# Scaling the softmax exponentials instead of the attention output, and turning operands amid the filler, in a banded-attention and MoE kernel

## The chip, the cores and the metric

The kernel runs on one core of a Trainium2 chip. The time is the device time of one execution in microseconds (us). Its engines appear in the profile as PE (matrix multiplications and transposes; PEld is its loading of weights), DVE (vector), ACT (scalar), POOL (GpSimd) and SP (which issues the transfers). Each engine takes its instructions strictly in its own program's order, and waits at an instruction until the semaphores that it names have been raised.

## The reference

Attention over 4 batches, 8 heads, 768 positions and a head size of 64: scores with a bias that falls with distance, kept for 8 global keys and the last 96 positions only, a softmax, and the product with the values. Its output (3072 rows of 512) goes through a mixture of 8 experts, whose gate is normalized by Sinkhorn steps.

```
scores = scale * np.matmul(q, k.transpose(0, 1, 3, 2)) + bias[None]
scores = np.where(keep, scores, -1000000000.0)
a = np.exp(scores - np.max(scores, axis=-1, keepdims=True))
a = a / (np.sum(a, axis=-1, keepdims=True) + 1e-09)
attn = np.matmul(a, v)
...
for e in range(E):
    out += P[:, e:e + 1] * (np.maximum(x @ w1[e], 0.0) @ w2[e])
```

## The kernel before

**Attention** (`Banded`) goes over 8 units of 384 positions (a batch's half). A unit has 4 pairs of heads, so there are 32 pairs `n`; a pair has 3 groups (one tile of 128 queries for two heads each), so there are 96 groups `t`. `unit` takes them two at a time, in six rounds per unit. I number the rounds of a unit 0 to 5. A round issues, in this order:

1. `ahead`: the scores `s_ps` of two groups four ahead of the round's own, and their softmax: on DVE a fused multiply, add and minimum into `p_sb` (L340), on ACT the exponentials with their sums (L344). After a pair's last group come the sum plus epsilon (L347), its inverse (L348), and a copy of it spread over 128 columns, `inv` (L350).
2. `flush`: the products with the values, `o_ps`, of the round before. If a pair ended, DVE multiplies `o_ps` by `inv` (L436), ACT rounds it to `xh` (L437, the tile `x`), and DVE takes the rest `xl` (L438).
3. `turn`: transposes of the round's own two groups into `t_ps`, copied to `pT` by ACT (L367).
4. `between(2)`, `between(1)`, `between(1)`: the round's **filler**. This is matmul work of the mixture's first expert for the unit before (`h_ps`, `y_ps`, and the gate's `g_ps` and `gt_ps`), drawn from a generator in step with the rounds. The argument sets how much is due, so half of it comes by the first call.
5. In rounds 1 and 4 `invert` for two pairs: three transposes each of `inv` into `r_ps`, copied back by DVE (L446). In rounds 0, 2, 3 and 5 `prepare`: a later pair's `q` and `k` are turned into two tiles `tp`, which ACT rounds to `qh` and `kh` (L295) and DVE reduces to `ql` and `kl` (L296).

PE's instructions are kept in program order; the order on ACT and DVE is set when the kernel is built, by a scheduler with a simulated timeline. The filler starts in round 1 of the second unit and takes the same shape in every unit: `y_ps` x6, `g_ps` x8 and `h_ps` x3 in round 1; `h_ps` x9, `gt_ps` x3 (the gate's transposes) and `h_ps` x6 in round 2; `h_ps` x18 in round 3; `h_ps` x12 and `y_ps` x6 in round 4; `y_ps` x12 in round 5 and in round 0 of the next unit.

**Buffers** of PSUM, all in use: `t_ps`, `tp`, `r_ps` and `gt_ps` share the tag "tp" with two buffers, taken in turn; the filler's `h_ps`, `y_ps` and `g_ps` share the tag "fl" with two (in the first unit `tp` and `r_ps` also take "fl"); `o_ps` has two, the scores one for each head. A tile waits until the tile two before it under the same tag has been read for the last time.

After attention come the remaining experts (`pipeline`, from L941 on), which the change doesn't touch: PE multiplies, and the other engines follow.

Of the kernel before, what the change touches and what calls it, by code (L numbers as in the profile page):

```python
# [8 lines left out]
F32 = mybir.dt.float32  # L9
# [3 lines left out]
ALU = mybir.AluOpType  # L13
# [4 lines left out]
P = 128  # L18
# [4 lines left out]
EPS = 1e-9  # L23
UT = 3
# [8 lines left out]
CHUNK = 2  # L33
LAG = 6
FG = 2
GROUPS = (((0, 0), (1, 0)), ((0, 1), (1, 1)), ((0, 2), (1, 2)))
# [79 lines left out]
class Banded:  # L116
# [184 lines left out]
    def scores(self, ts):  # L301
# [19 lines left out]
                    self.pe.matmul(s_ps, lhsT=t[m][0], rhs=t[m][1], start=(m == 0), stop=(m == 2))  # L321
        return s_lists

    def softmax(self, t, s_list):


        nc, D = self.nc, self.D
        n, group = divmod(t, len(GROUPS))
        _, half, g = self.work[n]
        p_sb = self.wrk.tile([P, 2, 2, P], F32, name="p_sb")  # L330
        mx = self.wrk.tile([P, 2], F32, name="mx", bufs=4)
        if group == 0:
            self.sums[n] = self.wrk.tile([P, UT, 2], F32, name="sm", bufs=4)
        sm = self.sums[n]
        views = []
        for u, (j, i) in enumerate(GROUPS[group]):
            h = 2 * g + j
            pv = p_sb[:, u, 0:len(KEYS[half][i])]
            views.append(pv)
            nc.vector.tensor_tensor_reduce(out=pv, in0=s_list[u], in1=self.bias(h, half, i), scale=-(D ** -0.5), scalar=3.0e38,  # L340
                                           op0=ALU.add, op1=ALU.min, accum_out=mx[:, u:u + 1])
        for u, pv in enumerate(views):
            j, i = GROUPS[group][u]
            nc.scalar.activation(out=pv, in_=pv, func=AF.Exp, bias=mx[:, u:u + 1], scale=-1.0,  # L344
                                 accum_out=sm[:, i, j:j + 1])
        if group == len(GROUPS) - 1:
            nc.scalar.add(sm, sm, EPS)  # L347
            nc.vector.reciprocal(out=sm, in_=sm)  # L348
            self.inv[n] = self.wrk.tile([P, UT, P], F32, name="inv", bufs=3)
            nc.scalar.copy(out=self.inv[n].rearrange("p t (j d) -> p (t j) d", j=2),  # L350
                           in_=sm.rearrange("p t j -> p (t j)").unsqueeze(2).broadcast_to([P, 2 * UT, D]))
        return p_sb
# [31 lines left out]
    def unit(self, u, xh, xl, between):  # L384

        NG, per = len(GROUPS), len(GROUPS) * (self.H // 2)
        if u == 0:
            self.load_k(2)  # L390
            self.prepare(0)
            self.load_v(0)
            self.scale_bias(0)
            self.keep_warm(self.ps, "o", WARM0)
            self.ahead(range(0, CHUNK))
            self.prepare(1)
            for g in range(1, self.H // 2):
                self.scale_bias(g)
            for t in range(CHUNK, AHEAD, CHUNK):
                self.ahead(range(t, t + CHUNK))  # L400
            self.prepare(2)
            self.load_v(2)
        for t in range(u * per, (u + 1) * per, CHUNK):
            self.ahead(range(t + AHEAD, t + AHEAD + CHUNK))
            self.flush()
            for t1 in range(t, t + CHUNK):
                n, group = divmod(t1, NG)
                if group == 0:
                    self.outs[n] = self.ps.tile([P, UT, P], F32, name="o_ps", tag="o", bufs=2)
                g = n % (self.H // 2)  # L410
                self.pending.append((n, group, self.turn(t1), self.outs[n], xh[g], xl[g]))
            for c in (CHUNK, 1, 1):
                between(c)
            n = t // NG
            if t % (2 * NG) == CHUNK:
                self.invert(n)
                self.invert(n + 1)
            else:
                self.prepare(n + NG)
        self.idle = None  # L420

    def flush(self):


        ended = None
        for n, group, pT, o_ps, xh, xl in self.pending:
            self.values(n, group, pT, o_ps)
            if group == len(GROUPS) - 1:
                ended = n, o_ps, xh, xl
        self.pending = []  # L430
        if ended is None:
            return
        n, o_ps, xh, xl = ended
        if n % 2:
            self.load_v(n + 3)
        self.nc.vector.tensor_tensor(out=o_ps, in0=o_ps, in1=self.inv.pop(n), op=ALU.mult)  # L436
        self.nc.scalar.copy(out=xh, in_=o_ps)  # L437
        self.nc.vector.tensor_tensor(out=xl, in0=o_ps, in1=xh, op=ALU.subtract)  # L438

# [687 lines left out]
```

## Time and profile before

| what | value |
|---|---|
| median of 3 runs | 2189.63 us (2189.43 to 2190.45) |
| the profiled execution's own time | 2190.28 us |
| its span, first to last instruction | 2188.4 us |
| PE, DVE, ACT, POOL busy | 99%, 61%, 35%, 51% |
| attention with filler under it | about 50 us to 295 us of the span |
| ACT busy from 60 to 295 us | 167.34 of 235 us |

Attention is the first seventh of the span; the rest is the mixture. PE's clock was granted in full throughout. A matmul's busy time overlaps that of the next, so the pace of PE is read from start to start in the timeline, not from the means. A round is recognized in the timeline by its twelve `s_ps`, then `o_ps`, then `t_ps`.

### The profile page before, as it was taken

How to read it: one execution, taken by the hardware profiler on the slowest of the kernel's cores; microseconds unless marked ns; L12 is line 12 of the kernel's file. 1: busy time of each engine (PE TensorE's matmuls, PEld its weight loads, DVE VectorE, ACT ScalarE, POOL GpSimd, SP SyncE). 2: the span in 40 equal slices, each digit the busy share in tenths (PEclk: the TensorE clock that was granted, in tenths of full speed). 3: DMA queues.
4: the chain of work that ended last, by engine and by line, in shares of the span. 5: the costliest groups of instructions: out<-in, count | busy, mean ns of one | idle time of the engine just before them, and what ended most of it. 6: DMA issues, size and time to landing. Idle time of an engine off the chain costs nothing.

```text
span 2188.4 us, 29227 instructions
## 1 busy us (share of the span) xinstructions
PE 2172.6 (99%) x10851; PEld 1807.7 (83%) x10851; DVE 1326.2 (61%) x2342; ACT 758.1 (35%) x1544; POOL 1124.3 (51%) x1053
## 2 busy tenths in 40 slices
PE   8999999999999999999999999999999999999998
PEld 6888888888888888888888888888888888888887
DVE  7555546665665665665666666666566566566565
ACT  7776753322322222223222223223233223222231
POOL 4858565554544544544544545545455545455440
PEclk9999999999999999999999999999999999999999
DMA  6666452111111111171111111111611111111111
GB/s 163 183 168 184 127 176 92 58 49 58 49 49 58 48 51 56 58 260 49 49 57 49 49 59 49 50 57 49 202 58 48 55 52 49 58 49 49 58 39 50
DMA packets 206280, 173.46 MB, mean 79 GB/s; under 512 B 101168, under 2 KB 169264, under 8 KB 206128
## 3 DMA queue, kind: packets, MB, share of 16 engines
q1 hardware_dynamic: 206128, 171.50, 25.3%
q8 instruction: 87, 1.43, 0.3%
q14 instruction: 65, 0.53, 0.1%
HBM read 142.36 MB, written 29.10 MB: 78 GB/s over the span
## 4 chain that ended last, share of the span: by engine, by line
PE 98%; ACT 1%; DVE 1%; DMA 0%; issue 0%; DVEq 0%; SPq 0%; ACTq 0%
PE y_ps L110 46%; PE bank_a L110 11%; PE bank_d L110 11%; PE bank_c L110 11%; PE bank_b L110 5%; PE h_ps L110 3%; PE o_ps L110 2%; PE s_ps L110 2%; PE t_ps L113 2%; PE tp L113 1%; PE r_ps L113 0%; PE g_ps L110 0%; ACT p_sb L344 0%; PE y_ps L736 0%; PE y_ps L735 0%; PE y_ps L737 0%
## 5 line engine op out<-in xcount | busy, mean ns | idle before, releaser
L1022 DVE SCALAR_TENSOR_TENSOR early<-y_ps,pm,early 128x512 f32<-128x512 f32 x672 | 502.9, 749 | 241.4 <-PE y_ps L110 240.9
L595 POOL TENSOR_TENSOR wl<-wsum,wh 128x1280 fp32r<-128x1280 f32 x90 | 266.5, 2961 | 577.3 <-ACT wh L594 577.3
L617 POOL TENSOR_TENSOR wsum<-w1f 128x256 f32<-128x256 f32 x450 | 317.5, 740 | 313.1 <-DMA w1f<-in_moe_w_dram 313.0
L110 PE MATMUL y_ps<-w2h,h_set 128*128 128x512 f32 x1408 | 433.5, 389 | 0.0
L110 PE MATMUL y_ps<-w2h,x 128*128 128x512 f32 x1408 | 433.5, 389 | 0.0
L594 ACT CAST w2h<-w2f 128x1024 fp32r<-128x1024 f32 x90 | 94.8, 1054 | 688.4 <-issue 619.0
L110 PEld LDWEIGHTS y_ps<-w2h,x 128*128 128x128 f32 x1408 | 264.3, 188 | 54.8
L110 PEld LDWEIGHTS y_ps<-w2h,h_set 128*128 128x128 f32 x1408 | 264.3, 188 | 54.8
L110 PE MATMUL y_ps<-w2l,h_set 128*128 128x512 f32 x704 | 274.1, 389 | 0.1
L110 PE MATMUL y_ps<-w2l,x 128*128 128x512 f32 x704 | 273.9, 389 | 0.0
L110 PE MATMUL bank_a<-m,wh 128*128 128x512 f32 x696 | 242.8, 389 | 1.0 <-DVE h_set L667 1.0
L110 PE MATMUL bank_d<-x,wh 128*128 128x512 f32 x696 | 242.6, 389 | 0.0
L110 PE MATMUL bank_c<-x,wh 128*128 128x512 f32 x696 | 242.5, 389 | 0.0
L595 POOL TENSOR_TENSOR w2l<-w2f,w2h 128x1024 fp32r<-128x1024 f32 x90 | 215.9, 2399 | 48.6 <-ACT w2h L594 48.6
L707 DVE TENSOR_TENSOR early<-early,bank_d 128x512 f32<-128x512 f32 x90 | 62.0, 689 | 175.6 <-PE bank_d L110 171.7
L110 PEld LDWEIGHTS y_ps<-w2l,h_set 128*128 128x128 f32 x704 | 132.2, 188 | 27.8 <-DVE early L1022 0.5
L110 PEld LDWEIGHTS y_ps<-w2l,x 128*128 128x128 f32 x704 | 132.2, 188 | 27.4
L110 PEld LDWEIGHTS bank_a<-m,wh 128*128 128x128 f32 x696 | 130.7, 188 | 29.0 <-DVE h_set L667 1.9
L110 PEld LDWEIGHTS bank_c<-x,wh 128*128 128x128 f32 x696 | 130.7, 188 | 27.1
L110 PEld LDWEIGHTS bank_d<-x,wh 128*128 128x128 f32 x696 | 130.6, 188 | 27.0
L110 PE MATMUL bank_a<-m,wl 128*128 128x512 f32 x348 | 135.4, 389 | 0.0
L110 PE MATMUL bank_d<-x,wl 128*128 128x512 f32 x348 | 135.4, 389 | 0.0
(228 smaller groups left out, 3473.6 us busy)
## 6 DMA issues: line engine op xcount, KB each, us to landing
w1f<-in_moe_w_dram SPq DMA_DIRECT2D x92, 512.0 KB, 3.5
w2f<-in_moe_w_dram SPq DMA_DIRECT2D x92, 512.0 KB, 3.3
x<-op_m SPq DMA_DIRECT2D x16, 512.0 KB, 7.4
op_m<-op SPq DMA_DIRECT2D x30, 256.0 KB, 2.5
m<-op_m SPq DMA_DIRECT2D x12, 512.0 KB, 7.0
out_dram<-early SPq DMA_DIRECT2D x24, 256.0 KB, 4.3
ys<-y_sb SPq DMA_DIRECT2D x21, 256.0 KB, 2.9
early<-ys SPq DMA_DIRECT2D x21, 256.0 KB, 4.1
```

The lines of the kernel that those rows point to most:

```text
L110: return self.tc.keep_in_program_order(self.engine.matmul(*args, **kw))
L113: return self.tc.keep_in_program_order(self.engine.transpose(*args, **kw))
L594: self.nc.scalar.copy(out=hi, in_=full)
L595: self.nc.gpsimd.tensor_tensor(out=lo, in0=full, in1=hi, op=ALU.subtract)
L617: nc.gpsimd.tensor_tensor(out=s[:, n], in0=x, in1=y, op=op)
L707: tt(out=t3, in0=t3, in1=d, op=ALU.subtract)
L1022: nc.vector.scalar_tensor_tensor(out=a, in0=y_ps, scalar=moe.pm[:, tt, e:e + 1], in1=a, op0=ALU.mult, op1=ALU.add)
```

## The change

The pairs of the first unit (`n < 4`) stay as they were. For every later pair, each group's two sums get epsilon and are inverted on DVE at once (two instructions on 128x2), and the exponentials themselves are multiplied by the inverse before they are turned: six multiplications per pair, of 128x256 (128x128 in a first group of a batch's first half), two on DVE (the first head of groups 0 and 2) and four on ACT. What they replace for those 28 pairs: the sum plus epsilon and `inv` on ACT, the six transposes per two pairs into `r_ps` on PE and their two copies on DVE, and the multiplication of `o_ps` on DVE.

Second, `prepare` moves from the end of the round to the middle of its filler, after `between(2)`.

```diff
+        early = self.early_pair(n)
+        if not early:
+            sm = self.wrk.tile([P, 2], F32, name="sm2", bufs=8)
+        elif group == 0:
             self.sums[n] = self.wrk.tile([P, UT, 2], F32, name="sm", bufs=4)
-        sm = self.sums[n]
...
-        if group == len(GROUPS) - 1:
+        if not early:
+            nc.vector.tensor_scalar(out=sm, in0=sm, scalar1=EPS, scalar2=None, op0=ALU.add)
+            nc.vector.reciprocal(out=sm, in_=sm)
+            for u, pv in enumerate(views):
+                if u == 0 and group != 1:
+                    nc.vector.tensor_scalar(out=pv, in0=pv, scalar1=sm[:, u:u + 1], scalar2=None, op0=ALU.mult)
+                else:
+                    nc.scalar.mul(pv, pv, sm[:, u:u + 1])
+        elif group == len(GROUPS) - 1:
+            sm = self.sums[n]
...
-            for c in (CHUNK, 1, 1):
-                between(c)
             n = t // NG
-            if t % (2 * NG) == CHUNK:
+            between(CHUNK)
+            if t % (2 * NG) != CHUNK:
+                self.prepare(n + NG)
+            elif self.early_pair(n):
                 self.invert(n)
                 self.invert(n + 1)
-            else:
-                self.prepare(n + NG)
+            between(1)
+            between(1)
...
-        self.nc.vector.tensor_tensor(out=o_ps, in0=o_ps, in1=self.inv.pop(n), op=ALU.mult)
+        if self.early_pair(n):
+            self.nc.vector.tensor_tensor(out=o_ps, in0=o_ps, in1=self.inv.pop(n), op=ALU.mult)
```

PE's order in round 2 of the second unit, before. `gt_ps` are the gate's transposes, `tp` the turned operands, `s_ps` opens the next round:

```order
L110 MATMUL h_ps<-x_174,w1h 128x384
L113 MATMUL gt_ps<-ident,g_sb 128x16 x3
L110 MATMUL h_ps<-x_175,w1h 128x384
L110 MATMUL h_ps<-x_173,w1l 128x384
L110 MATMUL h_ps<-x_173,w1h 128x384
L110 MATMUL h_ps<-x_175,w1h 128x384
L110 MATMUL h_ps<-x_173,w1l 128x384
L110 MATMUL h_ps<-x_173,w1h 128x384
L113 MATMUL tp<-ident,early 128x128 x6
L110 MATMUL s_ps_1146<-kl,qh 128x256
```

The same place in the changed kernel:

```order
L110 MATMUL h_ps<-x_174,w1h 128x384
L113 MATMUL tp<-ident,early 128x128 x6
L113 MATMUL gt_ps<-ident,g_sb 128x16 x3
L110 MATMUL h_ps<-x_175,w1h 128x384
L110 MATMUL h_ps<-x_173,w1l 128x384
L110 MATMUL h_ps<-x_173,w1h 128x384
L110 MATMUL h_ps<-x_175,w1h 128x384
L110 MATMUL h_ps<-x_173,w1l 128x384
L110 MATMUL h_ps<-x_173,w1h 128x384
L110 MATMUL s_ps_1169<-kl,qh 128x256
```

`tp` now stands ahead of `gt_ps`, which in the buffers' turn takes the first of the two `tp` tiles: its wait, which named ACT before, names DVE's `ql` now.

ACT's order in that round, before (`x` is the rounded attention output, `hh` belongs to the filler):

```order
L344 ACTIVATE p_sb,sm<-p_sb,mx 128x256 x4
L367 COPY pT<-t_ps 128x512
L437 CAST x_173<-o_ps 128x3x128
L347 ACTIVATE sm<-sm 128x6
L367 COPY pT<-t_ps 128x512
L666 ACTIVATE hh<-h_ps 128x384
L350 COPY inv<-sm 128x384
L295 CAST qh<-tp 128x384
L295 CAST kh<-tp 128x384
```

And in the changed kernel, where L350 are the exponentials, L453 is the rounding of the output, L382 the copies of `pT`, L359 the multiplications and L682 `hh`:

```order
L350 ACTIVATE p_sb,sm_1053<-p_sb,mx 128x256
L453 CAST x_173<-o_ps 128x3x128
L350 ACTIVATE p_sb,sm_1064<-p_sb,mx 128x256
L350 ACTIVATE p_sb,sm_1053<-p_sb,mx 128x256
L350 ACTIVATE p_sb,sm_1064<-p_sb,mx 128x256
L382 COPY pT<-t_ps 128x512 x2
L359 ACTIVATE p_sb<-p_sb,sm_1053 128x256
L682 ACTIVATE hh<-h_ps 128x384
L359 ACTIVATE p_sb<-p_sb,sm_1064 128x256
L295 CAST qh<-tp 128x384
L295 CAST kh<-tp 128x384
```

The rounding of the output moved ahead of both copies of `pT`, and the two multiplications stand between `pT` and `qh`.

More of the change, by code (lines that the diff above doesn't have):

```diff
@@ L322, in scores, with early_pair @@
         return s_lists
+    def early_pair(self, n):
+        return n < self.H // 2
     def softmax(self, t, s_list):
@@ L331, in softmax @@
         mx = self.wrk.tile([P, 2], F32, name="mx", bufs=4)
-        if group == 0:
+        early = self.early_pair(n)
+        if not early:
+            sm = self.wrk.tile([P, 2], F32, name="sm2", bufs=8)
+        elif group == 0:
             self.sums[n] = self.wrk.tile([P, UT, 2], F32, name="sm", bufs=4)
-        sm = self.sums[n]
         views = []
@@ L344, in softmax @@
             nc.scalar.activation(out=pv, in_=pv, func=AF.Exp, bias=mx[:, u:u + 1], scale=-1.0,
-                                 accum_out=sm[:, i, j:j + 1])
-        if group == len(GROUPS) - 1:
+                                 accum_out=self.sums[n][:, i, j:j + 1] if early else sm[:, u:u + 1])
+        if not early:
[8 more added lines that the diff above has]
+            sm = self.sums[n]
             nc.scalar.add(sm, sm, EPS)
             nc.vector.reciprocal(out=sm, in_=sm)
-            self.inv[n] = self.wrk.tile([P, UT, P], F32, name="inv", bufs=3)
+            self.inv[n] = self.wrk.tile([P, UT, P], F32, name="inv", bufs=2)
             nc.scalar.copy(out=self.inv[n].rearrange("p t (j d) -> p (t j) d", j=2),
```

## The prediction, made before the changed kernel ran

> **What bounds the kernel now.** I read the page first, its busy times and the chain that ended last, then the busy times of the stretch of attention that has filler under it, then the timeline of single rounds.
>
> ```profile
> span 2188.4 us, 29227 instructions
> PE 2172.6 (99%) x10851; PEld 1807.7 (83%) x10851; DVE 1326.2 (61%) x2342; ACT 758.1 (35%) x1544; POOL 1124.3 (51%) x1053
> PE 98%; ACT 1%; DVE 1%; DMA 0%; issue 0%; DVEq 0%; SPq 0%; ACTq 0%
> 60.00:295.00 235.00, 235.00 (x1994) 205.61 (x1990) 126.89 (x464) 167.34 (x526) 167.12 (x195) 1.00 0.59 164
> ```
>
> PE sets the end, and from 60 to 295 us it is never idle; ACT is busy there for 167.34 of 235 us (71%), DVE for 126.89 (54%). So what the change takes off PE is worth its full length, as long as PE still finds everything ready. Whether it does is a matter of single rounds. This is round 2 of a unit on PE, from the `r_ps` that close the round before to the next `s_ps`:
>
> ```profile
> 208.78 0.34 PE L110 MATMUL h_ps<-x,w1h 128*128 128x384 f32 x1
> 208.96 0.82 PE L113 MATMUL r_ps<-ident,inv 128*128 128x128 f32 x6
> 209.71 0.38 PE L110 MATMUL s_ps<-kl,qh 64*128 64x256 f32 x2
> ...
> 210.61 1.09 PE L110 MATMUL o_ps<-pT,early 128*64 128x128 f32 x16
> 211.63 1.09 PE L113 MATMUL t_ps<-ident,p_sb 128*128 128x128 f32 x8
> 212.48 0.42 PE L110 MATMUL h_ps<-x,w1h 128*128 128x384 f32 x1
> ...
> 213.99 0.34 PE L110 MATMUL h_ps<-x,w1h 128*128 128x384 f32 x1
> 214.25 0.35 PE L113 MATMUL gt_ps<-ident,g_sb 16*128 16x16 f32 x3
> ...
> 215.69 0.82 PE L113 MATMUL tp<-ident,early 128*128 128x128 f32 x6
> 216.44 0.39 PE L110 MATMUL s_ps<-kl,qh 64*128 64x256 f32 x2
> ```
>
> and the same round on ACT, and DVE's two rows that matter:
>
> ```profile
> 211.18 0.51 ACT L344 ACTIVATE p_sb<-p_sb,mx 128x256 f32<-128x256 f32 x1 [2.22 <-DVE mx L340]
> 211.69 0.49 ACT L344 ACTIVATE p_sb<-p_sb,mx 128x256 f32<-128x256 f32 x1
> ...
> 213.16 0.57 ACT L367 COPY pT<-t_ps 128x512 f32<-128x512 f32 x1
> 213.63 0.47 ACT L437 CAST x<-o_ps 128x384 fp32r<-128x384 f32 x1
> 214.00 0.21 ACT L347 ACTIVATE sm<-sm 128x6 f32<-128x6 f32 x1
> 214.11 0.57 ACT L367 COPY pT<-t_ps 128x512 f32<-128x512 f32 x1
> 214.57 0.49 ACT L666 ACTIVATE hh<-h_ps 128x384 fp32r<-128x384 f32 x1
> 214.96 0.51 ACT L350 COPY inv<-sm 128x384 f32<-128x384 f32 x1
> 216.22 0.48 ACT L295 CAST qh<-tp 128x384 fp32r<-128x384 f32 x1 [0.75 <-PE tp L113]
> ...
> 210.71 0.42 DVE L340 CUSTOM_DVE_ANT_1 p_sb<-s_ps,early 128x256 f32<-128x256 f32 x1 [0.20 <-PE s_ps L110]
> 216.73 0.56 DVE L296 TENSOR_TENSOR ql<-tp,qh 128x384 fp32r<-128x384 f32 x1 [1.07 <-ACT qh L295]
> ```
>
> What to see: counted from the round's start (209.71), the second `pT` is done at 4.97 us (214.68), `tp` comes at 5.98; a full microsecond of slack. And from `tp`'s start (215.69) it takes until 217.29, 1.60 us, for `qh` and `ql` to have read the first `tp` tile. In the old order the next round's scores and values run in that time.
>
> **The change part by part.** *The transposes of `inv`.* A filler step followed by `r_ps` and `s_ps` takes 208.78 to 209.71, 0.93 us. Without `r_ps` the same passage stands once in the trace, in the last unit, and takes 0.27 us:
>
> ```profile
> 294.65 0.34 PE L110 MATMUL h_ps<-x,w1h 128*128 128x384 f32 x1
> 294.92 0.39 PE L110 MATMUL s_ps<-kl,qh 64*128 64x256 f32 x2
> ```
>
> So 0.66 us for each of the 14 rounds that lose their `r_ps` (two in each of seven units): **-9.2 us**, all of it on the path. This is also all that can be gained, since PE waits for nothing there; what goes from DVE (two copies, one multiplication, one inverse) was hidden behind PE.
>
> *`tp` in mid-filler, ahead of `gt_ps` (round 2).* `tp` takes the two buffers of `t_ps`, and `gt_ps` right behind it takes the first `tp` tile's again, so PE must stand still until `ql` has read it. The floor is in the rows above: 1.60 us after `tp`'s start plus about 0.05 for the signal, where PE needs 0.65 for its six transposes: 1.0 us, if ACT takes `qh` at once. It won't, by its new order: one exponential, `x`, three exponentials, two `pT`, multiplication, `hh`, multiplication, `qh`. I put durations to it. The multiplication by a per-partition number isn't in the trace at this size; the nearest rows are the exponential, with such an operand too, and a rounding from SBUF without one:
>
> ```profile
> L344 ACT ACTIVATE p_sb<-p_sb,mx 128x256 f32<-128x256 f32 x160 | 80.0, 501 | 54.6 <-DVE mx L340 54.4
> L594 ACT CAST wh<-w1f 128x256 fp32r<-128x256 f32 x180 | 63.8, 404 | 0.0
> ```
>
> Between 404 and 501 ns I take 0.50 us, from the one with the operand, and a step of 0.40, because neighbours on ACT overlap by 0.1 (213.16 + 0.57 against 213.63). From the round's start: first exponential at 1.47; `x` at 2.10, when `o_ps` is done; three exponentials at 2.47, 2.96 and 3.45; `pT` at 3.94 and 4.40, done at 4.50 and 4.97; multiplication 4.87, `hh` 5.27, multiplication 5.66, `qh` 6.06 to 6.54, `ql` until 7.13, `gt_ps` at 7.18. PE reaches `tp` after nine `h_ps` at 4.46, is held by both `pT` for 0.24 in all, and reaches `gt_ps` at 5.35. The loss is 0.24 + 1.83 = 2.07 us; with exponentials of 128 columns, in every second unit, the same walk gives 1.74. Six rounds (units 2 to 7 of eight; the last has no operands left to turn) by 1.9: **+11.4 us**. Ends: 6 x 1.0 = 5.8 if ACT were free, and 18 if `qh` came another microsecond later.
>
> *`tp` in the other rounds (3, 5 and 0).* Here the first half of the filler is nine `h_ps` or six `y_ps`. In a round that started at 110.75, the seventh `y_ps`, in whose place `tp` comes now, stood at 4.04 us:
>
> ```profile
> 110.75 0.39 PE L110 MATMUL s_ps<-kl,qh 64*128 64x256 f32 x2
> 114.79 0.39 PE L110 MATMUL y_ps<-w2l,hh 128*128 128x512 f32 x1
> ```
>
> The second tile comes three transposes (0.33) later and needs the second `pT`, which by the steps above ends between 4.65 and 4.91, now that `x` stands ahead of it. That holds PE for 0.2 to 0.55, mean 0.35, in twelve rounds 5 and 0, and for 0.12 in six rounds 3: **+4.9 us**. Ends: 0, and 10 at 0.55 throughout. That PE does wait there when `pT` is late shows once in the first unit, where no filler stands between:
>
> ```profile
> 44.25 1.05 ACT L367 COPY pT<-t_ps 128x512 f32<-128x512 f32 x2
> 44.87 0.55 PE L113 MATMUL tp<-ident,raw_q 128*128 128x128 f32 x3 [1.25 <-ACT pT L367]
> ```
>
> *The multiplications ahead of `y_sb` (round 1).* `h_ps` after the gate's `g_ps` takes the buffer that `y_sb` has to empty. In the round that started at 202.61 this was already to the point:
>
> ```profile
> 207.69 0.58 ACT L894 COPY y_sb<-y_ps 128x512 f32<-128x512 f32 x1
> 208.33 0.44 PE L110 MATMUL h_ps<-x,w1h 128*128 128x384 f32 x1
> ```
>
> Now three multiplications, 1.2 us, stand ahead of `y_sb`, while the exponentials start some 0.4 earlier, because the casts of `tp` are mostly over. `y_sb` ends 0.5 to 0.75 later than `h_ps` needs: 0.6 in seven rounds, **+4.2 us**. Ends: 0 and 5.3.
>
> *The first unit's last rounds* have no filler, and ACT leads there. The second unit's first softmaxes fall into them: eight multiplications (3.2 us) come in, two sums and `inv` go (1.2). I take **+1.5 us**, between 0 and 3.2.
>
> *At nothing*: the small DVE instructions (per pair three sums plus epsilon and three inverses of about 0.18, two multiplications of 0.25 to 0.45, against 1.3 removed: L436, L446 and L348) add 0.5 us to a pair, stay under DVE's 54%, and in the walk they are done before 4.9, ahead of `qh`. The operands' loads are issued half a round earlier on SP, ahead of the spills that the second half of the filler queues; no wait of PE before names a transfer, and each load has two rounds or more. If that cover failed, PE would stand at `tp` for as long as the load is late, in each of 24 rounds.
>
> The sum: -9.2 + 11.4 + 4.9 + 4.2 + 1.5 = **+12.8 us**. The profiled execution took 2190.28 (span 2188.4 and 1.9 around it), 0.65 above the median; added to the median of 2189.63 this makes **2202.4 us**, 0.6% slower. [...]
>
> **The rivals.** *ACT keeps ahead* (same): `pT` and `qh` come as early as in the old order, say because `x` never holds ACT up. Then only the floor is left: -9.2 + 5.8 + about 1 = -2.4, 2187 us. For it: 29% of ACT is idle. Against: the idle time lies at the start of each round, ahead of the first exponential (the 2.22 us in the row), not ahead of `pT`.
>
> *The transposes go, and nothing takes their place* (faster): `gt_ps` doesn't have to wait for `ql`, because the casts finish under PE's own transposes. The place is round 2, the price 0.66 us in 14 rounds, 2181 us; it decides once all new waits together stay under 4.8 us. Against: 1.60 us of `qh` and `ql` cannot pass under 0.65 us of PE.
>
> *ACT becomes the bound*: four multiplications of 0.4 for each pair, less 0.6 for the sum and `inv`, add 1.0 us to a pair's 7.0 (167.34 over the 24 pairs of these six units, of 9.8 us each), 82%. If single rounds overflow into the next, the ends above apply: -9.2 + 18 + 8 + 5.3, about +22, 2212 us. Against: every round ends with idle time on ACT before it.
>
> **How the numbers follow.** Forecast 0.66 (2195 to 2209), ACT keeps ahead 0.16, nothing in the transposes' place 0.12, ACT the bound 0.06. A measurement of this kernel tells 0.2%, 4.4 us, from no change. Faster 0.12 and same 0.16 are the two middle rivals, slower 0.72 the forecast and the last. For 8 in 10 I go down to 2187, the floor's case, and up to 2212, the last's.
>
> **What would show it.** Right: in round 2, PE idle before `gt_ps` for 1 to 2 us, released by `ql`, six times; `tp` held by `pT` for tenths of a microsecond; `h_ps` after `g_ps` held by `y_sb`; PE's busy share from 60 to 295 us below full for the first time; no `r_ps` after 40 us. Wrong: `gt_ps` following `tp` within 0.3 us, or `qh` starting within 0.6 us of `tp`'s start in round 2, and a span that is shorter by about 9 us.

## The result, and the profile after

The changed kernel takes **2223.5 us** (median of 6 runs, 2221.28 to 2224.89), the one before 2189.70 (2189.43 to 2191.05, 6 runs). The ratio is 1.0151, with a 95% interval of 1.0141 to 1.0161: slower by 33.8 us. The forecast was slower too, but by 12.8 us, to 2202.4, with a range up to 2212.

From here on I count against the profiled execution, which took 2221.8 us; its span is 31.6 us longer than the one before (2220.0 against 2188.4). The changed kernel's page, its span, its busy times and its chain:

```profile
span 2220.0 us, 29286 instructions
...
PE 2180.6 (98%) x10767; PEld 1804.0 (81%) x10767; DVE 1378.0 (62%) x2482; ACT 786.0 (35%) x1600; POOL 1123.5 (51%) x1053
...
PE 93%; DVE 3%; ACT 3%; issue 1%; DMA 0%; SPq 0%; DVEq 0%; ACTq 0%
```

and the stretch with filler, in the same columns as before (us, busy times with instructions, then the granted clock):

```profile
60.00:295.00 235.00, 216.88 (x1725) 180.61 (x1726) 153.18 (x520) 167.91 (x506) 143.72 (x162) 0.96 0.52 147
```

PE was busy for all 235 us of this stretch before and is now for 216.88. What has no match in the prediction is the last number but two: the granted clock was 1.00 and is 0.96. The waits of the changed kernel's PE, by what was waited for (us in total, times, longest):

```profile
PE h_ps L110 <- ACT y_sb L910: 8.9, 6, 2.1
PE gt_ps L113 <- DVE ql L296: 8.9, 6, 1.7
PE tp L113 <- ACT pT L382: 5.7, 8, 3.5
```

Places and releasers are the predicted ones: `gt_ps` released by `ql` six times, `tp` by `pT`, `h_ps` by `y_sb`. The size of the first row is not, with waits up to 2.1 us where I had 0.6. Of the third row 3.5 us is a single wait in the first unit's last rounds (at 46.48; the same wait took 1.25 before); the other seven make 2.2.

The table compares every round of the units 1 to 7 with the same round before, by the starts of its `s_ps` in the two traces (us, summed over the units). "Predicted" are the terms of the prediction, put where they belong (the gain from the transposes goes half to round 1 and half to round 4). The other columns are the changed kernel and those experiments that a later section needs.

| round | predicted | changed | scaling alone | move alone | changed, no epsilon | the same, PE kept busy |
|---|---|---|---|---|---|---|
| 0 of unit 1 (no filler yet) | +1.5 | +2.8 | +2.7 | 0.0 | +2.9 | +4.0 |
| 0 (others) and 5 | +4.2 | +5.1 | +0.2 | +3.2 | +5.2 | +5.2 |
| 1 | -0.4 | +7.4 | +2.3 | -0.5 | +1.5 | +1.3 |
| 2 | +11.4 | +16.3 | +5.7 | +7.4 | +13.2 | +11.9 |
| 3 | +0.7 | +4.5 | +3.1 | +0.8 | +6.9 | +1.5 |
| 4 | -4.6 | -4.6 | -4.5 | -0.1 | -4.6 | -4.6 |
| difference of the spans | +12.8 | +31.6 | +9.8 | +10.3 | +25.1 | +19.2 |

**Round 2, where the stall was foreseen.** The rows of PE in the second unit, in a round that started at 55.07:

```profile
60.06 1.02 PE L113 MATMUL tp<-ident,early 128*128 128x128 f32 x6 [0.37 <-ACT pT L382]
62.67 0.37 PE L113 MATMUL gt_ps<-ident,g_sb 16*128 16x16 f32 x3 [1.58 <-DVE ql L296]
```

and ACT and DVE in the same round:

```profile
60.39 0.50 ACT L359 ACTIVATE p_sb<-p_sb,sm 128x256 f32<-128x256 f32 x1
60.80 0.46 ACT L682 ACTIVATE hh<-h_ps 128x384 fp32r<-128x384 f32 x1
61.17 0.49 ACT L359 ACTIVATE p_sb<-p_sb,sm 128x256 f32<-128x256 f32 x1
...
61.57 0.45 ACT L295 CAST qh<-tp 128x384 fp32r<-128x384 f32 x1
...
62.06 0.56 DVE L296 TENSOR_TENSOR ql<-tp,qh 128x384 fp32r<-128x384 f32 x1 [0.20 <-ACT qh L295]
```

Multiplication, `hh`, multiplication, `qh`, `ql`, `gt_ps`: the walk of the prediction, step by step. It had `qh` at 6.06 and `gt_ps` at 7.18 from the round's start; they stand at 6.50 and 7.60, because the exponentials began 0.4 later. The step on ACT is 0.40 (60.39, 60.80, 61.17, 61.57), as taken. But look at the clock in the 3.5 us behind `gt_ps` (the number to read is the third from the end):

```profile
62.90:66.40 3.50, 3.50 (x20) 3.02 (x19) 0.54 (x3) 0.00 (x0) 3.42 (x6) 0.52 0.29 75
```

and at the starts of the six `h_ps` there and of what follows them, in the changed kernel and then at the same place before:

```profile
62.97 0.69 PE L110 MATMUL h_ps<-x,w1h 128*128 128x384 f32 x1
...
65.19 0.58 PE L110 MATMUL s_ps<-kl,qh 64*128 64x256 f32 x2
```

```profile
214.54 0.45 PE L110 MATMUL h_ps<-x,w1h 128*128 128x384 f32 x1
...
215.69 0.82 PE L113 MATMUL tp<-ident,early 128*128 128x128 f32 x6
```

From 62.9 on PE is busy, but at half its clock, for about 3.4 us. The six `h_ps` take 2.22 us there, against 1.15 before and 1.25 in the changed kernel's next unit, where the clock stayed full (108.41 to 109.66). This stall was paid twice: 1.58 us while PE stood, and about 1 us more in the six `h_ps` behind it.

**Round 1, where the stall was three times the foreseen.** The rows of a round that started at 92.16, on DVE, POOL, ACT and PE:

```profile
95.22 1.30 POOL L655 TENSOR_TENSOR xres<-x 128x512 f32<-128x512 f32 x1
...
95.27 1.27 DVE L353 TENSOR_SCALAR sm<-sm 128x2 f32<-128x2 f32 x1 [0.54 <-ACT p_sb L350]
...
96.48 1.29 POOL L656 TENSOR_TENSOR xsum<-x 128x512 f32<-128x512 f32 x1
96.58 0.17 DVE L354 RECIPROCAL sm<-sm 128x2 f32<-128x2 f32 x1
96.78 1.06 DVE L357 TENSOR_SCALAR p_sb<-p_sb,sm 128x128 f32<-128x128 f32 x1
...
97.77 0.15 DVE L353 TENSOR_SCALAR sm<-sm 128x2 f32<-128x2 f32 x1
...
98.16 0.91 ACT L359 ACTIVATE p_sb<-p_sb,sm 128x256 f32<-128x256 f32 x2 [0.91 <-DVE sm L354]
98.97 0.56 ACT L910 COPY y_sb<-y_ps 128x512 f32<-128x512 f32 x1
...
99.59 0.44 PE L110 MATMUL h_ps<-x,w1h 128*128 128x384 f32 x1 [2.08 <-ACT y_sb L910]
```

The sum plus epsilon on DVE, an addition to two numbers per partition, took 1.27 us. It ended at 96.54, where POOL's addition that had started just ahead of it ended too (96.52). The multiplication behind it took 1.06, until POOL's next one was done. The next sum started at 97.77, when POOL had just ended, and took 0.15. The reciprocal beside it took 0.17 each time, whatever POOL did. So it is in the whole trace: of the 84 sums, the 35 that began while POOL was idle took 155 to 171 ns, and the 49 that began while POOL was in an instruction ended 24 to 63 ns after that instruction did. ACT's multiplications waited 0.91 us for the inverse, `y_sb` stood behind them, and PE stood 2.08 us. The groups of these three over the whole run (the count, busy time, mean ns of one):

```profile
L353 DVE TENSOR_SCALAR sm<-sm 128x2 f32<-128x2 f32 x84 | 38.7, 461 | 15.3 <-ACT p_sb L350 14.6
L357 DVE TENSOR_SCALAR p_sb<-p_sb,sm 128x256 f32<-128x256 f32 x44 | 26.7, 608 | 1.3
L354 DVE RECIPROCAL sm<-sm 128x2 f32<-128x2 f32 x84 | 13.9, 165 | 2.6
```

I had put about 0.18 us for the sum and 0.25 to 0.45 for the multiplication. So there were two candidates for the missing 19 us: DVE's new instructions, which seem to wait for POOL, and PE's half pace after a stall.

### The profile page after: what moved, and what is told of

Same layout as the page of the kernel before. It is cut to its first block, busy times and chain, and to the rows that moved or that the text cites. A ratio compares the mean times of both kernels' runs of the same rounds, so it can differ in the third digit from the quotient of the medians.

```text
span 2220.0 us, 29286 instructions
## 1 busy us (share of the span) xinstructions
PE 2180.6 (98%) x10767; PEld 1804.0 (81%) x10767; DVE 1378.0 (62%) x2482; ACT 786.0 (35%) x1600; POOL 1123.5 (51%) x1053
## 4 chain that ended last, share of the span: by engine, by line
PE 93%; DVE 3%; ACT 3%; issue 1%; DMA 0%; SPq 0%; DVEq 0%; ACTq 0%
PE y_ps L110 45%; PE bank_a L110 11%; PE bank_d L110 11%; PE bank_c L110 11%; PE bank_b L110 5%; PE h_ps L110 2%; PE s_ps L110 2%; ACT p_sb L350 1%; PE o_ps L110 1%; PE t_ps L113 1%; PE tp L113 1%; DVE sm L353 1%; DVE p_sb L357 1%; ACT pT L382 0%; DVE p_sb L346 0%
```

## The experiments

The experiments ran in four groups, each beside the kernel before on the same chip (medians of 2190.05 to 2190.62 us there).

### The scaling alone

The operands are turned at the round's end, as before; the scaling is that of the changed kernel.

```diff
             between(CHUNK)
+            between(1)
+            between(1)
             if t % (2 * NG) != CHUNK:
                 self.prepare(n + NG)
...
-            between(1)
-            between(1)
```

> The early scaling alone: the operands are turned at the end of the round again, as before. Theory A (DVE's new instructions that read and write SBUF alone wait for POOL's, and so the copy of y_sb comes late): the removed transposes give -9.2 us, the waits of h_ps for y_sb in round 1 stay at 10 to 12, the first unit costs 3: 2190 to 2200 us, and the small instructions on DVE still take up to 1.3 us. Theory B (ACT's own added work makes y_sb late, as the prediction had it): -9.2 + 4.2 + 1.5, 2186 us.

Measured: 2199.57 us, ratio 1.0039 (1.0025 to 1.0053), in theory A's range, but not by its way. The scaling alone loses 10 us, though it takes 9.2 us of transposes off PE. PE's largest wait in the whole trace, and its place in a round 2:

```profile
PE tp L113 <- issue: 4.3, 2, 2.2
```

```profile
99.13 1.12 DVE L353 TENSOR_SCALAR sm<-sm 128x2 f32<-128x2 f32 x1
...
100.17 1.44 DVE L357 TENSOR_SCALAR p_sb<-p_sb,sm 128x256 f32<-128x256 f32 x1
...
101.71 1.17 DVE L357 TENSOR_SCALAR p_sb<-p_sb,sm 128x128 f32<-128x128 f32 x1
102.80 0.17 DVE L785 COPY lg<-gt_ps 128x24 f32<-128x24 f32 x1
...
103.29 0.63 PE L113 MATMUL tp<-ident,early 128*128 128x128 f32 x4 [2.16 <-issue]
```

Here `y_sb` was in time (the scheduler had put it ahead), where theory A had 10 to 12 us of waits for it. The loss came out elsewhere. The largest piece: the gate's `lg` (L785, L786), which has to empty the buffer of `gt_ps` for the second `tp`, stood on DVE behind three of the new instructions, 1.1 to 1.4 us each. The row names no releaser, so that it is `lg` is read from DVE's order and the times: `tp` starts when `lg`'s two instructions, from 102.80 on, are over. A stretch at half clock follows each of these two stalls (granted clock 0.50 from 104.5 and from 186.4 us on), and `t_ps` waits another 3.7 us for `kl`, behind DVE as well.

### The move alone

`prepare` amid the filler, with the output scaled through `inv` as before and `invert` at the round's end. The edit is against the kernel before:

```diff
-            for c in (CHUNK, 1, 1):
-                between(c)
             n = t // NG
+            between(CHUNK)
+            if t % (2 * NG) != CHUNK:
+                self.prepare(n + NG)
+            between(1)
+            between(1)
             if t % (2 * NG) == CHUNK:
                 self.invert(n)
                 self.invert(n + 1)
-            else:
-                self.prepare(n + NG)
```

> The turning of the operands amid the filler alone, without the early scaling; the inverse sums are turned at the end of their rounds as before. Theory A (PE runs at half pace for some 3.5 us after an idle time of more than about a microsecond): gt_ps waits 1.0 to 1.4 us in six rounds and PE then loses about 1.5 more, tp waits 0.1 to 0.4 in 18 rounds: 2207 to 2213 us, granted clock below full behind each gt_ps. Theory B (the waits are all there is): 2199 to 2203 us.

Measured: 2200.68 us, ratio 1.0049 (1.0032 to 1.0065): theory B held. PE's first wait and the rows of one round 2:

```profile
PE gt_ps L113 <- DVE ql L296: 5.4, 6, 0.9
```

```profile
96.62 1.14 PE L113 MATMUL tp<-ident,early 128*128 128x128 f32 x7
...
97.42 0.49 ACT L295 CAST qh<-tp 128x384 fp32r<-128x384 f32 x1
98.05 0.55 DVE L296 TENSOR_TENSOR ql<-tp,qh 128x384 fp32r<-128x384 f32 x1
...
98.65 0.35 PE L113 MATMUL gt_ps<-ident,g_sb 16*128 16x16 f32 x3 [0.89 <-DVE ql L296]
```

With no multiplication on ACT, `gt_ps` waits 0.9 us each time: the floor of 1.0 that the prediction worked out. The granted clock stays at 1.00 from 60 to 295 us, so a stall of 0.9 us brought no half pace. Each part alone costs 10 to 11 us, together they cost 34; some 14 us come from their meeting.

### The changed kernel without POOL's sums and differences

This one leaves out POOL's additions and subtractions of activations for the later experts, so those experts compute something else; the amount of work on the other engines stays.

```diff
-            moe.combine((new[:, 0], new[:, 1]), block(x, c, n), block(y, c, n), op, xtmp)
-            spills.append((op_spill[b][m][:, :, q], new))
+            spills.extend((op_spill[b][m][:, s, q], block(x, c, n)[s]) for s in range(2))
```

> The changed kernel without POOL's sums and differences of the attention output (the tiles are spilled as they are, so the first layer's operands are not the sums that the mixture needs). Theory A (POOL holds DVE's new instructions up): L353 falls to about 0.17 us and L357 to 0.35, the waits of h_ps for y_sb fall from 9.9 to 4 us or less, the first unit gets 2 us back: 2213 to 2217 us. Theory B (ACT's work alone): 2222 to 2225 us, waits unchanged.

Measured: 2213.71 us, ratio 1.0106 (1.0089 to 1.0123), in theory A's range. The group of the sums, and the wait for `y_sb`:

```profile
L353 DVE TENSOR_SCALAR sm<-sm 128x2 f32<-128x2 f32 x84 | 17.9, 213 | 18.7 <-ACT p_sb L350 17.6
```

```profile
PE h_ps L110 <- ACT y_sb L908: 2.3, 6, 0.6
```

The mean of a sum falls from 461 to 213 ns (the first unit's weights are still made on POOL, under which one of them took 2.3 us), `y_sb`'s waits from 8.9 to 2.3 us, longest 0.6: that is the size that the prediction had for this term. So POOL's work is what made DVE's instructions long, and that made `y_sb` late. 24 us of loss remain, and the half pace with them: round 3 still loses 6.9 us.

### The changed kernel with PE kept busy at the stall

Twelve useless transposes follow `tp` in round 2, into a part of `tp` that nobody reads, so that PE does not stand still before `gt_ps`.

```diff
-    def prepare(self, n):
+    def prepare(self, n, extra=0):
...
+            for _ in range(extra if hi is kh else 0):
+                self.pe.transpose(out=tp[:, 3], in_=src[:, nb - 1], identity=self.ident)
...
-                self.prepare(n + NG)
+                self.prepare(n + NG, 12 if t > 4 * NG and t % (4 * NG) == 2 * CHUNK else 0)
```

> The changed kernel with 12 useless transposes (1.3 us) behind tp in each round 2, in the time in which PE waits for gt_ps anyway; the wait itself still ends with ql. Theory A (PE's half pace follows from its idle time): h_ps behind gt_ps runs at full pace, 1.3 to 1.8 us less in six rounds: 2213 to 2216 us. Theory B (the half pace has another cause): 2222 to 2226 us.

Measured: 2218.59 us, ratio 1.0127 (1.011 to 1.0143), between the two ranges: 5 us less than the changed kernel, with more work on PE, where theory A had at least 7.5. Round 3 lost 1.5 us in place of 4.5, 0.22 to 0.26 in each unit. The stretch with filler:

```profile
60.00:295.00 235.00, 223.41 (x1814) 187.04 (x1813) 153.37 (x528) 170.80 (x516) 144.77 (x163) 0.98 0.53 150
```

The clock is at 0.98 in place of 0.96: the half pace behind `gt_ps` is gone, and two stretches of it remain, each behind a stall of 2.1 us for `y_sb` in round 1.

### All multiplications on ACT

The scaling alone again (operands turned at the round's end), without the sum plus epsilon (a softmax's sum is at least 1, the exponential of its own maximum, so 1e-9 changes no bit of it in fp32), and with DVE's two multiplications of a pair on ACT.

```diff
-            nc.vector.tensor_scalar(out=sm, in0=sm, scalar1=EPS, scalar2=None, op0=ALU.add)
             nc.vector.reciprocal(out=sm, in_=sm)
             for u, pv in enumerate(views):
-                if u == 0 and group != 1:
-                    nc.vector.tensor_scalar(out=pv, in0=pv, scalar1=sm[:, u:u + 1], scalar2=None, op0=ALU.mult)
-                else:
-                    nc.scalar.mul(pv, pv, sm[:, u:u + 1])
+                nc.scalar.mul(pv, pv, sm[:, u:u + 1])
```

> As the scaling alone (operands turned at the round's end again, 2199.57 us), but without the sum plus epsilon (a softmax's sum is at least 1, so 1e-9 changes nothing in fp32), and with all six multiplications of a pair on ACT. DVE keeps only the reciprocal, which took 0.16 us throughout and waited for nobody on POOL. Theory (what the scaling alone loses comes from DVE's two new forms, which wait behind POOL's instruction and hold up lg, ql and the exponentials' scaling): the losses of rounds 1, 2 and 3 go, round 4's gain of 3.9 us stays, the first unit still costs 1 to 3 us: 2186 to 2191 us, and the wait of tp for the gate's buffer in round 2 (4.3 us) is under 1. Rival (ACT's load is the cause: 56 more multiplications of 0.4 us come on to ACT): rounds 1 to 3 lose as much as before or more, with PE waiting for y_sb or pT: 2198 to 2206 us.

Measured: 2205.25 us, ratio 1.0069 (1.0052 to 1.0086). The theory's number fell and the rival's held: rounds 2 and 3 were free of loss (0.0 us each), as the theory had it, but rounds 1, 4 and 0 lost 4.1, 5.4 and 5.5. PE waits at the start of a round now:

```profile
66.39 1.70 ACT L355 ACTIVATE p_sb<-p_sb,sm 128x256 f32<-128x256 f32 x4
...
67.98 0.48 ACT L678 ACTIVATE hh<-h_ps 128x384 fp32r<-128x384 f32 x1
...
68.35 0.48 ACT L295 CAST qh<-tp 128x384 fp32r<-128x384 f32 x1
...
70.69 1.09 PE L113 MATMUL t_ps<-ident,p_sb 128*128 128x128 f32 x8 [1.29 <-DVE ql L296]
```

Four multiplications (1.70 us) stand ahead of `hh` and `qh` on ACT, `ql` then falls behind DVE's work for the next scores, and the next round's `t_ps` finds its buffer still read. So in this order ACT has no room for six multiplications a pair.

### The same on the changed kernel

The same edit of the scaling, with `prepare` amid the filler.

> As the changed kernel (2223.5 us, operands turned amid the filler), with the same edit of the scaling: no sum plus epsilon, all six multiplications on ACT. Theory (two causes that multiply each other: the transposes' place costs 1 to 1.7 us at gt_ps in six rounds, whatever scales the exponentials; DVE's waits behind POOL make y_sb late): the waits for y_sb fall from 8.9 us to under 4, the loss of round 1 from 7.4 to under 3, that of round 2 stays at 10 to 16, since more multiplications stand ahead of qh: 2206 to 2216 us. Rival (ACT's load): no better than the changed kernel, 2222 to 2232 us.

Measured: 2218.98 us, ratio 1.0133 (1.0117 to 1.015), in neither range. `y_sb`'s waits fell to 1.7 us and round 1 lost 0.1 in place of 7.4, as the theory had it, but round 2 lost 18.0, more than its 16: ACT had all six of a pair's multiplications instead of four, and `gt_ps` waited 14.0 us in all, up to 2.5 at a time.

### Only the sum plus epsilon left out

The scaling alone, with one line less.

```diff
-            nc.vector.tensor_scalar(out=sm, in0=sm, scalar1=EPS, scalar2=None, op0=ALU.add)
             nc.vector.reciprocal(out=sm, in_=sm)
```

> As the scaling alone (2199.57 us), with only the sum plus epsilon left out; the two multiplications of a pair on DVE stay. Theory: every sum plus epsilon waits behind POOL's instruction (mean 0.46 us against 0.15 undisturbed, 84 of them), the multiplications too (mean 0.61, 56 of them); taking the first away takes about half of the loss in rounds 1 to 3 away (10 us): 2192 to 2197 us. If only the multiplications matter: 2198 to 2200; if only the sums: 2187 to 2191.

Measured: **2189.72 us**, ratio 0.9997 (0.9988 to 1.0007): 9.9 us less than the scaling alone, as much as that had lost on balance, from one instruction on two numbers per partition. My theory had half; the number is that of its third case, that only the sums matter. The multiplications still wait:

```profile
L356 DVE TENSOR_SCALAR p_sb<-p_sb,sm 128x256 f32<-128x256 f32 x44 | 32.8, 746 | 1.5
```

At 746 ns they are even longer than in the changed kernel (608). The difference, as I read the order of the instructions, is what stands behind: the sum is the first link for all of a group's multiplications, ACT's too, while DVE's own multiplication only holds what DVE has next. That is argued, not tried, and it isn't free everywhere: in the first unit's last rounds two multiplications of 1.56 and 2.25 us stand on DVE ahead of the next scores' work (from 40.16 on), `pT` comes late, and PE waits 3.5 us for it. Round 1 has none of the transposes' gain either. The version that beats both, below, gets both back.

### Another instruction in the sum's place

It could still be any further instruction at that point that costs 10 us. So here a useless reciprocal of the same two numbers, into a scratch tile, stands in the place of the sum.

```diff
-            nc.vector.tensor_scalar(out=sm, in0=sm, scalar1=EPS, scalar2=None, op0=ALU.add)
+            nc.vector.reciprocal(out=self.wrk.tile([P, 2], F32, name="sm3", bufs=8), in_=sm)
             nc.vector.reciprocal(out=sm, in_=sm)
```

> As the scaling alone without the sum plus epsilon (2189.72 us), but with a useless instruction in its place: a reciprocal of the same 128x2 numbers into a scratch tile. So DVE has as many instructions in as long a chain as in the scaling alone (2199.57 us), and only the form differs: a reciprocal took 0.16 us throughout, the sum plus epsilon 0.46 on average, up to 1.25, when POOL was busy. Theory (it is the form, which waits behind POOL): 2189 to 2192 us. Rival (any further instruction between the exponentials and their scaling costs it, by its place in DVE's order): 2197 to 2201 us. Between: both.

Measured: 2189.35 us, ratio 0.9995 (0.9986 to 1.0005). The theory held. The two groups of reciprocals:

```profile
L354 DVE RECIPROCAL sm<-sm 128x2 f32<-128x2 f32 x84 | 13.8, 165 | 2.5
L353 DVE RECIPROCAL sm<-sm 128x2 f32<-128x2 f32 x84 | 13.7, 163 | 22.0 <-ACT p_sb L350 21.1
```

Same size, same count, same place in DVE's order; 163 ns in place of 453, and 10 us of the kernel. One thing differs besides the form: nothing reads this reciprocal's result, while the sum's was the next instruction's input. With that proviso, it is the form of the instruction, together with POOL's work beside it.

### All multiplications on ACT, and y_sb on DVE

```diff
-                    nc.scalar.copy(out=y_sb, in_=y_ps)
+                    nc.vector.tensor_copy(out=y_sb, in_=y_ps)
```

> As e5_scale_act, with y_sb copied from PSUM by DVE, which takes 0.6 us off ACT for each of the first expert's tiles; a copy out of PSUM should not wait for POOL. Theory (DVE's forms were the cause, and ACT is only tight behind pT): no PE wait for y_sb or y_ps, 2182 to 2189 us, below the kernel before by up to 0.3%. Rival (y_sb on DVE waits behind DVE's longer work, as lg did): PE waits at h_ps behind g_ps for 0.5 us or more in each round 1: 2191 to 2196 us.

Measured: 2192.67 us, ratio 1.0012 (1.0002 to 1.0021). With `y_sb` off ACT the kernel is 12.6 us faster than with all multiplications alone, and no wait for `y_sb` is left; rounds 0 lose 1.3 in place of 5.5, and round 1 gains 3.6 where it lost 4.1. But `t_ps` still waits for `ql` behind ACT's multiplications, 7.5 us in six rounds 4, so the theory's range was missed by nearly 4 us. The number lies in the rival's range, but not by the rival's way: `y_sb` is in time.

### A version that beats both

From these: the scaling alone, without the sum plus epsilon, with `y_sb` copied on DVE, and the old way also for the second unit's first two pairs, whose scaling falls into the first unit's rounds where ACT leads.

```diff
     def early_pair(self, n):
-        return n < self.H // 2
+        return n < 3 * self.H // 4
...
-                    nc.scalar.copy(out=y_sb, in_=y_ps)
+                    nc.vector.tensor_copy(out=y_sb, in_=y_ps)
```

> As the scaling alone without the sum plus epsilon (2189.72 us), with two edits more: the old way also for the second unit's first two pairs, whose scaling falls into the first unit's rounds where ACT leads (the loss there was 3.2 + 0.9 + 0.6 us), and y_sb copied from PSUM by DVE, which took 3.6 us off round 1 when all multiplications were on ACT. Theory: the first unit's loss falls to under 1 us, less 0.7 for its r_ps; round 1 gains 2 to 4; round 4's gain of 4 stays: 2181 to 2186 us, faster than the kernel before by 0.2 to 0.4%. Rival (y_sb behind DVE's multiplications, which still wait for POOL, comes late): PE waits at h_ps behind g_ps, 2187 to 2192.

Measured: **2182.60 us** (5 runs, 2182.43 to 2183.13), ratio 0.9966 (0.9952 to 0.9979). The theory held: 0.34% faster than the kernel before, 41 us faster than the changed one. The first unit's loss is gone. The busy times of its page (the span is 2180.5 us):

```profile
PE 2164.4 (99%) x10773; PEld 1799.2 (83%) x10773; DVE 1354.9 (62%) x2415; ACT 773.3 (35%) x1575; POOL 1125.2 (52%) x1053
```

Rounds 1 and 4 have the transposes' gain, -4.4 and -4.6 us; round 2 gives 1.2 back. This is nearly what the rival "the transposes go, and nothing takes their place" had promised (2181), but only with the operands turned at the round's end.

### The changed kernel without the sum plus epsilon

> The changed kernel (2223.5 us) with only the sum plus epsilon left out. Theory (the prediction's terms held, and the sum's wait behind POOL was what they lacked, at y_sb and, by PE's half pace after the longer stalls, behind gt_ps): 2200 to 2208 us, with y_sb's waits under 4 us, gt_ps's at 8 to 11, and a granted clock of 0.99 or more in each round. Rival (the multiplications on DVE, which wait too, or ACT's order are enough for the late y_sb): 2214 to 2222 us.

Measured: 2213.19 us, ratio 1.0103 (1.0088 to 1.0119), between the two ranges. One line less gives 10.3 us back here too. The waits and the clock:

```profile
PE gt_ps L113 <- DVE ql L296: 9.5, 6, 1.7
...
PE h_ps L110 <- ACT y_sb L909: 3.2, 6, 0.6
```

```profile
60.00:295.00 235.00, 221.28 (x1766) 183.59 (x1766) 129.89 (x467) 170.91 (x519) 147.38 (x168) 0.96 0.54 150
```

The waits are those of the theory, 3.2 for `y_sb` and 9.5 for `gt_ps`; its clock is not. I had thought that the half pace would go with the long stalls for `y_sb`. It stays at 0.96, with five stretches after the first unit behind the stalls at `gt_ps` alone, of 1.5 to 1.7 us.

### Both causes taken away

The changed kernel without the sum plus epsilon, and with the twelve useless transposes behind `tp` in round 2.

> The changed kernel without the sum plus epsilon (2213.19 us), and PE kept busy behind tp in round 2 by twelve useless transposes into a part of tp that nobody reads, as in the run with the busy wait alone (2218.59 us against 2223.5 for the changed kernel). Both causes that the prediction lacked are then taken away: the sums' wait behind POOL, and PE's half pace after it stood still. Theory (nothing else is missing from the prediction's sum): the transposes fill most of gt_ps's wait without adding to it, the waits for y_sb stay at 0.6 us each, no half pace after the first unit, and the time comes near the 2202.4 us predicted: 2200 to 2207 us. Rival (the half pace isn't caused by the idle time at gt_ps, or there is a third cause): 2210 to 2216 us.

Measured: 2208.91 us, ratio 1.0082 (1.0066 to 1.0099), 2 us above the theory's range and 1 below the rival's. The clock and the waits:

```profile
60.00:295.00 235.00, 228.76 (x1881) 190.46 (x1881) 133.94 (x482) 177.85 (x540) 153.42 (x174) 1.00 0.54 152
```

```profile
PE tp L113 <- ACT pT L383: 6.2, 7, 4.3
PE h_ps L110 <- ACT y_sb L911: 3.2, 6, 0.6
...
PE gt_ps L113 <- DVE ql L298: 1.7, 6, 0.4
```

No half pace after the first unit, and the rounds of the units behind the second come out at the predicted size: round 2 loses 1.8 to 2.0 (predicted 1.9), round 3 loses 0.25, rounds 0 and 5 lose 0.2 to 0.65 (0.2 to 0.55). What is still too long lies in the last rounds of the first unit and the first of the second, for which the sum had 1.5 in all: `tp` waits 4.3 us for `pT` once, 3.1 more than before, and PE runs at half pace from 45.8 to 52.6 us, in the last part of that wait and behind it.

## Why the prediction was wrong, point by point

**The sign and the places were right.** All four waits that the prediction named are there, with the releasers it named, and no other of size. The rivals on the fast side fell: PE did wait for `ql`. "ACT becomes the bound" fell too, though its 2212 lies nearest: the share of ACT that it priced, 82%, is reached in the scaling alone without the sum plus epsilon (192.42 of the 235 us), and that kernel takes 2189.72.

**The removed transposes** (-9.2 us, 0.66 a round): round 4 gained 0.65 to 0.68 in every unit (0.57 once), in the changed kernel and in each experiment that scales the exponentials, but for the two with all multiplications on ACT and the operands at the round's end. Right.

**`gt_ps` behind `ql`** (+11.4): right as a mechanism, with ACT's order and its steps of 0.40. In the changed kernel it measures 9 to 10 us of waits (8.9 of idle time in the view), and round 2 loses 11.9 with both other causes gone. The floor, 0.9 measured for 1.0, is the move alone.

**`tp` held by `pT`** (+4.9, of which 4.2 in rounds 0 and 5): rounds 0 and 5 lost 5.1 us, within the bounds, but only in part by this way. PE was idle for 1.9 of the 5.1. Every second round 5 lost 0.21 with PE never idle, and with both other causes gone each round 3 loses 0.22 to 0.25 in the same manner. So breaking the filler's run with `tp` costs some 0.2 us in such a round, a term that the sum didn't have; what makes it was not tried. That the total came out is partly luck.

**`y_sb` behind the multiplications** (+4.2, ends 0 and 5.3): 9.9 us of waits, counted from start to start (8.9 of idle time in the view), outside the ends. With the sum plus epsilon gone, or POOL's work, the view has 2.3 to 3.2, 0.6 at the longest. So the walk was right and an input of it wrong.

**That input is the step that failed: "At nothing: the small DVE instructions", "about 0.18" for the sum and 0.25 to 0.45 for the multiplication.** The durations came from rows of other forms (a reciprocal of 184 ns), and the cover from DVE's 54%. The new forms took 461 and 608 ns on average, up to 1.29 and 2.20 us, because they did not get done while an instruction of POOL's ran: each of the 49 sums that began during one ended 24 to 63 ns after it. A busy share doesn't show that. The trace of before could not price it, having no such instruction in attention, but it did show POOL busy for 167.12 of the 235 us, and I did not bound the term from both sides as I did the others. An estimate of the upper end, from that trace's POOL instructions of 128x512 (1.28 to 1.29 us on average): 1.3 us for each of 12 sums and 8 multiplications of a unit would have been 26 us of DVE in a unit.

**The second missing term is the clock.** The sum counted each stall once. In the changed kernel six stretches of 3.41 us behind the first unit run at half clock. From `gt_ps` to the next round's `o_ps` PE takes 3.91 and 3.94 us where such a stretch follows (62.67, 151.16), and 2.44 and 2.46 where none does (108.13, 196.66). So a stretch costs about 1.5 us, and the six of them 9. The same comes out as a remainder. The lengthened steps at the waits are 31.3 us by the terms below; less 9.2 for the transposes that makes 22.1 of the 31.0 us at the end of attention, and leaves 8.9. That the stall is the cause at `gt_ps` is shown by the two runs with PE kept busy there, of which one lost 5 us less and the other 4 us less than without. "PE's clock was granted in full throughout" held from 60 to 295 us of a kernel in which PE never stood there; even that kernel's trace has half clock early on, from 14.3 to 17.7 us.

**The first unit** (+1.5, between 0 and 3.2): 2.8 us in round 0 of the second unit, 4.0 with both other causes gone (the account below puts 3.6 on it, since the half pace there reaches into the next round). There POOL makes weights, and DVE's multiplication stood behind it for 2.20 us. (The change also gave `inv` two buffers in place of three; the fastest version has two as well and loses nothing here.)

In sum, at the end of attention: predicted 12.8; `y_sb` +5.7, `gt_ps` -1.5, `tp` and the short waits beside it +3.0, the first unit +2.1, half pace +8.9; 31.0 measured. The pieces for `y_sb` to the first unit are lengthened steps counted from start to start in the trace, good to about 1 us, the breaks of the filler's run and the first unit's own half pace among them; the half pace is what is left over, and the six stretches give the same.

## What to carry to other kernels

Ask of each added instruction not only how long it is and whether its engine has room, but what it may have to wait for on the engines beside it. Here, on DVE, a multiplication or addition with a number from SBUF to SBUF waited for POOL (up to 2.20 and 1.29 us in place of 0.36 and 0.17), a reciprocal of 128x2 (0.16 to 0.17 us on average) or a subtraction that reads PSUM (0.54 to 0.56 us with POOL busy) did not, and where the waiting instruction is the first link of a chain, its wait is everybody's. On a PE that otherwise never stands still, a new stall can cost its own length and then some 1.5 us in clock, as 23 of the 29 stalls of 1.38 us or more in these runs brought on half pace and none of the 43 of up to 1.34 us; fill it, or keep it short. And moving work earlier is no gain by itself: the operands turned amid the filler brought their buffer's wait in front of `gt_ps`, which had waited for nobody.

## What the runs showed of the hardware

**DVE and POOL.** In the changed kernel a sum of 128x2 took 155 to 171 ns when POOL was idle at its start (35 of 84), and otherwise until 24 to 63 ns after POOL's instruction had ended (49 of 84, up to 1289 ns). A multiplication of 128x256 took 345 to 357 ns when POOL was idle at its start (17 of 44), and otherwise until 0.15 to 0.84 us after POOL's instruction had ended (27 of 44, up to 2203 ns). Reciprocals of 128x2 took 163 to 166 ns on average in the changed kernel and ten of the experiments, and 33 of the changed kernel's 84 began while POOL was busy. The subtractions into `ql`, which read PSUM and SBUF, took 0.54 to 0.56 us with POOL busy at their start and 0.52 to 0.56 with POOL idle. `y_sb` from PSUM on DVE took 686 ns on average in the fastest version, with no wait of PE for it.

**PE's clock after a stall.** In the changed kernel and ten of the experiments, PE stood for 0.9 us or more at 72 places between 57 and 340 us. None of the 43 stalls of up to 1.34 us brought on half pace (one fell into a stretch that was already running). Of the 29 of 1.38 to 3.9 us 23 did; it began during the stall or at most 1.9 us after its end, and lasted 3.41 us or twice or three times that. The six without one are stalls of 1.38 to 2.17 us, so length alone does not decide. What goes with it shows in the traces, for the most part. In each of them all changes of the clock lie on one grid of 3.41 us (in the changed kernel 62.87, 66.28, 100.42, 103.83, 151.62 and so on). From 57 to 330 us the fourteen traces have 1105 cells of their grids at full clock. In 26 of them PE was idle for 1.38 us or more in all, and 23 were followed by a cell at half clock; of the 1079 with less idle time none was. Five of the six stalls without half pace lie across a border of the grid, with no more than 1.30 us of idle time in either cell. The sixth had 1.64 in one cell, and stays open.
